# A three-stage kernel on one core: the last group's input combinations and the gate later, seven output pairs parked in HBM, two temporaries elsewhere

## The chip, the core and the metric

The kernel runs on one core of a Trainium2 chip. A core has TensorE (PE in the profile, with its weight loads as PEld), VectorE (DVE), ScalarE (ACT), GpSimd (POOL) and SyncE (SP, which here only issues DMAs). Each engine executes its own list of instructions in order and waits at semaphores for the others. The metric is the device time of one execution in microseconds (us). Three runs of the kernel before took 2025.17, 2027.48 and 2030.88 us, so the median is 2027.48 us.

## What is computed

Three layers follow each other on 2304 tokens of 512 values: a windowed attention, a rational two-layer network, and a mixture of 8 experts. The change lies in the third, of which the reference is:

```
logits = x @ w_gate                       # 2304 x 8
P = np.exp(logits - logits.max())
for _ in range(8):                        # the gate: rows and columns made even in turn
    P /= P.sum(1, keepdims=True) + 1e-09
    P /= P.sum(0, keepdims=True) + 1e-09
    P *= N / E
out = 0
for e in range(8):
    h = np.maximum(x @ w1[e], 0.0)        # 512 -> 1024
    ye = h @ w2[e]                        # 1024 -> 512
    out += P[:, e:e + 1] * ye
```

Every expert works on every token. P only scales the expert's output by rows, so the matrix products can begin before P is known; the scaled sum can't.

## The kernel before, in words

The tokens of the third layer form three groups G of 768. A visit v is one expert on one group; there are 24, experts outermost, the group order turning round at each expert (0 1 2, 2 1 0, ...). A visit has four steps m, each with a quarter of the hidden values, so there are 96 steps. Both matrix products use Strassen-like combinations: seven products take the place of eight. Each number is held as two 16-bit halves, so each product is three matmuls.

- **First layer** (`moe_l1`, matmuls at L925, banks `l1a` and `l1b`): step m has seven products at positions 0 to 6. One product is a unit u of the program: six matmuls of 384 columns. The units number 672, and 28 more follow for the second layer. ScalarE (L974, L981) and VectorE (L976, L979, L984) take results out of the two banks, VectorE and GpSimd combine them (L947), ScalarE rounds them to 16 bits (L991) and VectorE writes the rest (L992) to a tile `hs0` to `hs5`. A position that uses a bank again must wait until the result before it has been taken out.
- **Second layer** (`moe_l2`, matmuls at L1016 to L1018 of 256 columns, four banks `yps`): it begins 28 units later. After 28 products of three matmuls an output pair is complete (two blocks of 128 tokens). `y_evac` (L1036 to L1041) takes it out of the banks to one of two tiles, `yd0` and `yd1`, in turn. There are 72 pairs. The next pair needs the same four banks.
- **Output** (`y_out`): two ScalarE scalings by columns of P (L1050), then a store for expert 0 (L1053, SP's queue) or an adding DMA for the others (L1055, GpSimd's queue). Scaling needs the gate. Until the gate is done the pairs stand in a list, `pend`, and keep `yd0` and `yd1`.
- **Gate**: `x2_logits` (L766, L768 on TensorE) for each group, then `gate_exp`, eight times `gate_iter` (L787 to L796 on VectorE, with one column sum on TensorE, L180, read at L191), `gate_done` (L801).
- **Inputs**: the seven combinations of a group's x are made by `mix_sub` (L744) and `mix_put` (L222 and L225), written to HBM (`xd`, L754) and read from there (L911) as the steps need them. `x2f` held two combinations that later ones are made of.
- **Weights**: raw expert weights come in through two buffers (L838 and L844 to L846), are searched for their largest value (L850), combined (L874) and split into halves (L885, L888).

`at_u(u, f)` puts a piece of work at unit u of the program as written; a scheduler then orders each engine's list. All big tiles lie at fixed places (`homes`) in a few large rooms (`roomA`, `roomV`, `roomIG` in the profile), so two tiles at one place must wait for each other.

Of the kernel before, what the change touches and what calls it, by code (L numbers as in the profile page):

```python
# [10 lines left out]
F32 = mybir.dt.float32  # L11
F32R = mybir.dt.float32r
F16 = mybir.dt.float16
# [15 lines left out]
def kernel(  # L29
# [67 lines left out]
    homes(homes(homes(0, 7168, "w1s4", "V1", 2), 6144, "E03a", "V1", 2), 4096, "yd1", "V1", 2)  # L97
    homes(0, 10752, "hs0 hs1 hs2", "V2", 2)
    homes(0, 6144, "E47", "IG", 2)
    homes(7168, 3072, "mix4 mix5", "V0", 2)  # L100
    homes(0, 3072, "mix6 mix7", "V1", 2)
    rooms = {}
# [90 lines left out]
    def delayed(fn, k):  # L193
        return fn() if k == 0 else lambda: delayed(fn, k - 1)
# [539 lines left out]
            )  # L734

    def mix_src(G, c):
        if c in (CT1, CT2):
            return room("x2f", [P, 2, XQ], F32)[:, c == CT2, :]
        n, h = {CX00: (0, 0), CX10: (0, 1), CT4: (0, 1), CT3: (1, 0), CX11: (1, 1)}[c]
        return xhome(2 * G + n)[:, h * XQ:(h + 1) * XQ]  # L740
# [210 lines left out]
    def moe_unit(u):  # L951
        m, pos = divmod(u, 7)
        if pos == 1:
            m -= 1
        if not 0 <= m < NM:
            return
        if pos == 0:
            mac[m] = dict(
                A=bank("l1a"), E=room("E03" + "ab"[m % 2], [P, 4, TB], F32), D=room("E47", [P, 4, TB], F32),
            )  # L960
        d = mac[m]
        if pos == 3:
            d["Y"] = bank("l1b")
        ps = d["Y" if pos in (1, 3, 5) else "A"]
        if pos in (0, 3, 5):
            d[pos] = dict(ps=ps, used=0, guests=[])
        group = d[{0: 0, 2: 0, 4: 0, 6: 0, 3: 3, 5: 5, 1: 5}[pos]]
        moe_l1(m, pos, ps[:, 0:TB], group)
        if pos in (0, 5):
            fresh[:] = [group]  # L970
        ps = ps[:, 0:TB]
        E = d["E"]
        if pos in (0, 2, 4):
            nc.scalar.activation(E[:, (0, 2, 3)[pos // 2], :], ps, AF.Copy)  # L974
        elif pos == 3:
            nc.vector.tensor_tensor(out=E[:, 0, :], in0=ps, in1=E[:, 0, :], op=ALU.add)  # L976
            nc.scalar.activation(E[:, 0, :], E[:, 0, :], AF.Relu)
        elif pos == 5:
            nc.vector.tensor_tensor(out=E[:, 3, :], in0=ps, in1=E[:, 3, :], op=ALU.add)  # L979
        elif pos == 6:  # L980
            nc.scalar.activation(E[:, 1, :], ps, AF.Relu)  # L981
            combine(m, 6, 1, 0, ALU.subtract)
        else:
            nc.vector.tensor_tensor(out=E[:, 2, :], in0=ps, in1=E[:, 2, :], op=ALU.add)  # L984
            nc.scalar.activation(E[:, 2:4, :], E[:, 2:4, :], AF.Relu)  # L985
            combine(m, 4, 0, 2, ALU.add)
            combine(m, 5, 4, 1, ALU.subtract)
            combine(m, 7, 3, 5, ALU.subtract)
            h = d["h"] = room(f"hs{m % 6}", [P, 2, 7, TB], F16)
            for src, o in ((E[:, 1:4, :], slice(0, 3)), (d["D"], slice(3, 7))):  # L990
                behind["a"] = nc.scalar.activation(h[:, 0, o, :], src, AF.Copy).ins.name  # L991
                behind["v"] = nc.vector.tensor_tensor(out=h[:, 1, o, :], in0=src, in1=h[:, 0, o, :], op=ALU.subtract).ins.name  # L992
# [36 lines left out]
    def y_evac(v, p):  # L1029
        yd = room(f"yd{(3 * v + p) % 2}", [P, 2, DM], F32)  # L1030
        vv = room("yv", [P, EH], F32)
        p1, p6, _, _, _, _, p4 = (yb[b][:, h * EH:(h + 1) * EH] for b, h, _, _ in PRODS)
        p75, p23 = (yb[b].rearrange("p (n c) -> p n c", n=2) for b in (1, 2))
        q4 = yd.rearrange("p n (h c) -> p (n h) c", h=2)
        w, z, u, x = (q4[:, i, :] for i in range(4))
        nc.scalar.activation(u, p1, AF.Copy)  # L1036
        nc.vector.tensor_tensor(out=vv, in0=p6, in1=u, op=ALU.add)
        nc.vector.tensor_tensor(out=q4[:, 0:4:3, :], in0=p75, in1=vv.unsqueeze(1).to_broadcast([P, 2, EH]), op=ALU.add)
        nc.vector.tensor_tensor(out=z, in0=p75[:, 0, :], in1=x, op=ALU.add)  # L1039
        nc.vector.tensor_tensor(out=q4[:, 2:4, :], in0=p23, in1=q4[:, 2:4, :], op=ALU.add)  # L1040
        nc.vector.tensor_tensor(out=w, in0=p4, in1=w, op=ALU.add)  # L1041
        if gate_ready[0]:
            y_out(v, p, yd)
        else:
            pend.append((v, p, yd))

    def y_out(v, p, yd):
        e, G = GV[v]
# [5 lines left out]
        else:  # L1054
            later_u.append((unit_now[0] + 2, lambda: pin("p", nc.gpsimd.dma_start(out=dst, in_=yd, accum_op=ALU.add))))  # L1055

    def flush_pend():
        gate_ready[0] = True
        for a in pend:
            y_out(*a)  # L1060
        pend.clear()


    LAG = 3
    ATT = ((1, 0, 7), (2, 7, 23), (3, 40, 62))
# [67 lines left out]
    def at_u(u, fn, *a):  # L1133
        at(4 * NS1 + int(2 * u), fn, *a)
# [10 lines left out]
    def mix_at(G, when, s0, slot0):  # L1145
        for dt, c, slot in zip(s0, (CX00, CX10, CT1, CX11, CT2, CT3, CT4), (0, 1, 2, 3, 0, 1, 2)):
# [1 line left out]
                when(dt, mix_sub, G, c)  # L1148
            when(dt, mix_put, G, c, slot0 + slot)
            if c == CX11:  # L1150
                when(dt + (0.5 if G < 2 else 2), x2_logits, G)

    def at_step(t, fn, *a):
        at(int(4 * t) + 1, fn, *a)

    mix_at(0, at_step, (56, 57, 58, 59, 61, 62, 63), 0)
    mix_at(1, at_step, (69, 70, 71, 72, 74, 75, 76), 0)
    mix_at(2, at_u, (9, 12, 15.5, 19, 27.5, 30, 32.5), 4)
    for c in range(7):
        at_step(78 + c // 3, x_load, 0, c)  # L1160
    at_step(80.5, x_load, 1, CX00)

    at_u(23.5, gate_exp)
    for u in (26, 29, 32, 35, 38, 41, 44, 47):
        at_u(u, gate_iter)
    at_u(49, gate_done)
    at_u(49.5, flush_pend)

    use = []

# [174 lines left out]
```

## Time and profile before

| what | value |
|---|---|
| median of three runs | 2027.48 us |
| profiled execution, its own time | 2025.65 us |
| its span, first to last instruction | 2023.9 us |
| TensorE busy, share of the span | 1896.6 us, 94% |
| VectorE busy | 1625.1 us, 80% |
| ScalarE busy | 1235.8 us, 61% |
| GpSimd busy | 486.8 us, 24% |
| mean granted TensorE clock | 0.968 |
| first and last matmul of the first expert layer | 633.0 and 1986.2 us |

The third layer takes the span from 633 us to its end. A busy time says how long an engine had something to do; a matmul's record is longer than the distance to the next matmul, because they overlap, so TensorE's rate is read from counts and distances of starts, not from its busy share.

### The profile page before, as it was taken

What the parts mean: (1) busy time and instruction counts of PE and PEld (TensorE: products, weight loads), DVE (VectorE), ACT (ScalarE), POOL (GpSimd) and SP (SyncE); (2) the same over time, 40 slices, a digit from 0 to 9 for tenths busy, and PEclk for the clock granted to TensorE, in tenths of its full rate; (3) what the DMA queues carried; (4) which work ended last, traced back from release to release, by engine and by line L of the source; (5) the groups of instructions that cost most, each with busy time, mean ns of one, the idle gap of its engine ahead of it and who ended that gap; (6) DMA issues with size and microseconds to landing.
All of it is one profiled execution on the core that took longest, in us unless ns stands there. A gap on an engine that the chain in (4) does not pass through costs nothing. (4 is left out here: it accounts for less than half of the span.)

```text
span 2023.9 us, 36375 instructions
## 1 busy us (share of the span) xinstructions
PE 1896.6 (94%) x13914; PEld 1428.6 (71%) x13914; DVE 1625.1 (80%) x2784; ACT 1235.8 (61%) x2328; POOL 486.8 (24%) x490
## 2 busy tenths in 40 slices
PE   7688899998989789999999999999999999999997
PEld 6466667876766566777777777777777777777776
DVE  5898899899998878778877877878778787787754
ACT  5777777776776536565654655556566466565543
POOL 1232233222222003112411511421231241141111
PEclk7688999999999899999999999999999999999999
DMA  6642220124310333146346345435534634543323
GB/s 174 167 142 77 60 75 14 33 65 143 105 41 12 120 105 110 62 127 160 72 109 170 67 104 144 110 62 135 154 64 107 175 78 105 152 87 79 87 55 47
DMA packets 209791, 200.06 MB, mean 99 GB/s; under 512 B 78288, under 2 KB 160208, under 8 KB 209616
## 3 DMA queue, kind: packets, MB, share of 16 engines
q1 hardware_dynamic: 192480, 164.70, 26.9%
q0 software_dynamic: 17136, 33.03, 10.9%
q8 instruction: 109, 1.79, 0.4%
q14 instruction: 66, 0.54, 0.1%
HBM read 151.67 MB, written 46.01 MB: 98 GB/s over the span
## 5 line engine op out<-in xcount | busy, mean ns | idle before, releaser
L925 PEld LDWEIGHTS <-roomA 128*128 128x128 f16 x3276 | 321.9, 99 | 197.6 <-issue 32.2
L925 PE MATMUL l1a<-roomA 128*128 128x384 f16 x1872 | 358.8, 328 | 4.8 <-ACT roomV L974 3.7
L925 PE MATMUL l1b<-roomA 128*128 128x384 f16 x1404 | 277.3, 329 | 14.1 <-DVE roomA L976 6.7
L683 POOL TENSOR_TENSOR roomIG<-roomA,roomIG 128x384 fp32r<-128x384 f32 x96 | 112.2, 1169 | 289.2 <-ACT roomIG L682 214.8
L947 POOL TENSOR_TENSOR roomIG<-roomA 128x384 f32<-128x384 f32 x48 | 60.7, 1264 | 464.4 <-ACT roomA L981 314.1
L1016 PE MATMUL yps<-roomA,roomV 128*128 128x256 f16 x630 | 170.3, 274 | 2.0 <-DVE roomV L1039 1.3
L1016 PE MATMUL yps<-roomA 128*128 128x256 f16 x630 | 169.6, 273 | 2.5 <-DVE roomV L1040 1.5
L1017 PE MATMUL yps<-roomA,roomV 128*128 128x256 f16 x630 | 171.5, 274 | 0.0
L1017 PE MATMUL yps<-roomA 128*128 128x256 f16 x630 | 170.8, 273 | 0.0
L1018 PE MATMUL yps<-roomA,roomV 128*128 128x256 f16 x630 | 170.6, 274 | 0.0
L1018 PE MATMUL yps<-roomA 128*128 128x256 f16 x630 | 169.4, 273 | 1.0 <-DVE roomA L992 1.0
L645 PE MATMUL h1ps<-roomA 128*128 128x384 f16 x384 | 131.5, 343 | 15.4 <-DVE roomA L665 7.9
L698 PE MATMUL o1ps<-roomIG,roomV 128*128 128x384 f32 x384 | 137.1, 357 | 4.3 <-POOL roomIG L683 4.1
L874 POOL TENSOR_TENSOR roomA<-roomA 128x256 f32<-128x256 f32 x140 | 130.1, 948 | 37.3 <-DVE roomA L888 23.6
L646 PE MATMUL h1ps<-roomA 128*128 128x384 f16 x384 | 130.7, 340 | 0.0
L699 PE MATMUL o1ps<-roomIG,roomV 128*128 128x384 f32 x384 | 130.6, 340 | 0.0
L888 DVE SCALAR_TENSOR_TENSOR roomA<-roomA,sm 128x768 f16<-128x768 f32 (+1 forms) x92 | 113.7, 1249 | 21.1 <-ACT roomA L885 19.8
L647 PE MATMUL h1ps<-roomA 128*128 128x384 f16 x384 | 130.4, 339 | 0.0
L947 POOL TENSOR_TENSOR roomIG<-roomV 128x384 f32<-128x384 f32 x48 | 50.0, 1041 | 323.5 <-ACT roomV L981 304.7
L697 PE MATMUL o1ps<-roomIG,roomV 128*128 128x384 f32 x384 | 106.1, 377 | 15.9 <-ACT roomIG L682 14.2
L1016 PEld LDWEIGHTS <-roomA 128*128 128x128 f16 x1008 | 98.6, 98 | 30.6 <-DVE roomA L1040 3.7
L1017 PEld LDWEIGHTS <-roomV 128*128 128x128 f16 x1008 | 99.0, 98 | 25.0 <-issue 1.5
(221 smaller groups left out, 5081.6 us busy)
## 6 DMA issues: line engine op xcount, KB each, us to landing
roomA<-xd SPq DMA_DIRECT2D x119, 384.0 KB
roomA<-in_moe_w_dram SPq DMA_DIRECT2D x256, 128.0 KB
roomA<-in_moe_w_dram SPq DMA_DIRECT2D x128, 256.0 KB
out_dram<-roomV POOLq DMA_DIRECT2D x32, 512.0 KB, 6.0
out_dram<-roomA POOLq DMA_DIRECT2D x31, 512.0 KB, 6.1
roomV<-in_moe_w_in_dram SPq DMA_DIRECT2D x16, 512.0 KB
roomA<-in_moe_w_out_dram SPq DMA_DIRECT2D x16, 512.0 KB
xd<-roomA SPq DMA_DIRECT2D x14, 384.0 KB
```

The lines of the kernel that those rows point to most:

```text
L645: mm = nc.tensor.matmul(hp, whi, xb[:, 0, kk, :], start=kk == 0, stop=False)
L646: nc.tensor.matmul(hp, whi, xb[:, 1, kk, :], start=False, stop=False)
L647: nc.tensor.matmul(hp, wlo, xb[:, 0, kk, :], start=False, stop=kk == KD - 1)
L683: nc.gpsimd.tensor_tensor(out=gl, in0=g, in1=gh.bitcast(F32), op=ALU.subtract)
L698: nc.tensor.matmul(ob[dd], hi, d["gl"], start=False, stop=False)
L699: nc.tensor.matmul(ob[dd], lo, d["gh"], start=False, stop=last)
L874: pin("p" if pool else "v", eng.tensor_tensor(out=d[:, o, :], in0=a, in1=b, op=ALU.add if w == 0 and n == 0 else ALU.subtract))
L888: pin("v", nc.vector.scalar_tensor_tensor(out=l, in0=x, scalar=sc, in1=h, op0=ALU.mult, op1=ALU.subtract))
L925: mm = nc.tensor.matmul(ps, w[:, wx_, wh, kk * P:(kk + 1) * P], x[:, xh, kk, :], start=start and kk == 0 and wh == 0 and xh == 0, stop=sto ...
L1016: nc.tensor.matmul(o, hh[:, a - 1, c], w[:, m, 0, :], start=i == 0 and half == 0, stop=False)
L1017: nc.tensor.matmul(o, hh[:, a - 1, c], w[:, m, 1, :], start=False, stop=False)
L1018: nc.tensor.matmul(o, hl[:, a - 1, c], w[:, m, 0, :], start=False, stop=i == NP - 1 and (half == 1 or b == 3))
```

## The change

- `x2t1` and `x2t2` are new tiles for the two helper combinations of the last group, in place of `x2f`; one lies where `mix0` and `yd0` lie, the other where `yd1` lies.
- The units of the last group's seven combinations move a little (9 to 10, 12 to 13, 15.5 to 17, 19 to 21, 27.5 to 26, 32.5 to 34), and its logits from 2 to 5 units behind the fourth.
- The gate starts at unit 36 in place of 23.5, its eight turns stand at 41 to 89 in place of 26 to 47, and it is done at 94 in place of 49.
- Each output pair that is complete before the gate is stored unscaled to a tile `yh` in HBM at once. From unit 97 on, half a pair at a time, it is read back to one tile `yr`, scaled by ScalarE and stored to the output. There are seven such pairs and so fourteen turns, two in seven units.
- The tiles `hs4` and `hs5` change their order of use.

```diff
+    homes(0, 3072, "x2t1")
+    homes(13312, 3072, "x2t2", "V1", 2)
+    homes(14336, 2048, "yr", "V0", 2)
...
+        if c in (CT1, CT2) and G == 2:
+            return room("x2t2" if c == CT2 else "x2t1", [P, XQ], F32)
...
-            h = d["h"] = room(f"hs{m % 6}", [P, 2, 7, TB], F16)
+            h = d["h"] = room(f"hs{(0, 1, 2, 3, 5, 4)[m % 6]}", [P, 2, 7, TB], F16)
...
-            pend.append((v, p, yd))
+            i = len(pend)
+            nc.sync.dma_start(out=yh[:, 2 * DM * i:2 * DM * (i + 1)], in_=yd.rearrange("p n c -> p (n c)"))
+            pend.append((v, p, i))
...
-    def flush_pend():
+    yh = hbm.tile([P, 8 * 2 * DM], F32, tag="yh", name="yh")
+
+    def flush_one(k):
+        v, p, i = pend[len(pend) - 1 - k // 2]
+        n = k % 2
+        e, G = GV[v]
+        assert e == 0
+        yr = room("yr", [P, DM], F32)
+        pin("a", nc.sync.dma_start(out=yr, in_=yh[:, DM * (2 * i + n):DM * (2 * i + n + 1)]))
+
+        def done():
+            pin("a", nc.scalar.activation(yr, yr, AF.Copy, scale=gate_col(e, 2 * TPB * G + TPB * n + p)))
+            nc.sync.dma_start(out=bass.AP(out.tensor, (2 * TPB * G + TPB * n + p) * P * DM, [[DM, P], [1, DM]]), in_=yr)
+
+        return delayed(done, 5)
+
+    def flush_pend(u):
         gate_ready[0] = True
-        for a in pend:
-            y_out(*a)
-        pend.clear()
+        for k in range(2 * len(pend)):
+            at_u(u + 2 + 7 * (k // 2) + 3 * (k % 2), flush_one, k)
...
-                when(dt + (0.5 if G < 2 else 2), x2_logits, G)
+                when(dt + (0.5 if G < 2 else 5), x2_logits, G)
...
-    at_u(23.5, gate_exp)
-    for u in (26, 29, 32, 35, 38, 41, 44, 47):
+    at_u(36, gate_exp)
+    for u in (41, 47, 53, 65, 71, 77, 83, 89):
         at_u(u, gate_iter)
-    at_u(49, gate_done)
-    at_u(49.5, flush_pend)
+    at_u(94, gate_done)
+    at_u(95, flush_pend, 95)
```

In the changed kernel the line numbers of the pieces below are 3 higher up to the gate's column sum (L191 becomes L194), and 5 higher from the logits to the second layer (L766 becomes L771, L1016 becomes L1021). L1051 is the store to `yh`, L1072 the load of `yr`, L1076 the store to the output.

TensorE's list at the last group's logits before, from the last logit matmuls of 16 columns on:

```order
L766 LDWEIGHTS roomV_6434
L766 MATMUL lgps<-wg,roomV_6434 128x16
L768 LDWEIGHTS roomV_6434
L768 MATMUL lgps<-wg,roomV_6434 128x8
L768 LDWEIGHTS roomV_6434
```

and the same place now (`yps` are the banks of the second layer):

```order
L771 LDWEIGHTS roomV_6435
L771 MATMUL lgps<-wg,roomV_6435 128x16
L1022 LDWEIGHTS roomV_6694
L1022 MATMUL yps<-roomA,roomV_6694 128x256
L773 LDWEIGHTS roomV_6435
L773 MATMUL lgps<-wg,roomV_6435 128x8
```

Matmuls of the second layer now stand between the logits; before, the first of them stood behind the gate's first column sum. From the logits to position 3 of step 4 there are 42 of them now and none before.

VectorE's list at the gate's first turns before (`gs` and `gt` are the gate's tiles):

```order
L888 SCALAR_TENSOR_TENSOR roomA<-roomA,sm 128x4x256
L191 TENSOR_SCALAR gs<-smps 128x8
L992 TENSOR_TENSOR roomA<-roomIG,roomA 128x1536
L794 RECIPROCAL gs<-gs 128x8
L795 TENSOR_SCALAR gs<-gs 128x8
L796 TENSOR_TENSOR gt<-gt,gs 128x144
L787 TENSOR_REDUCE gs<-gt 128x18
L788 TENSOR_SCALAR gs<-gs 128x18
L789 RECIPROCAL gs<-gs 128x18
L790 TENSOR_TENSOR gt<-gt,gs 128x144
L792 TENSOR_REDUCE gs<-gt 128x8
```

and in the first turn now (L1042 to L1046 take out the first output pair):

```order
L795 TENSOR_TENSOR gt<-gt,gs 128x144
L1042 TENSOR_TENSOR roomA<-yps,roomA 128x256
L797 TENSOR_REDUCE gs<-gt 128x8
L1043 TENSOR_TENSOR roomA<-yps,roomA 128x2x256
L981 TENSOR_TENSOR roomV_6584<-l1b,roomV_6584 128x384
L1044 TENSOR_TENSOR roomA<-yps,roomA 128x256
L1046 TENSOR_TENSOR roomA<-yps,roomA 128x256
L997 TENSOR_TENSOR roomA<-roomIG,roomA 128x1536
L984 TENSOR_TENSOR roomA<-l1b,roomA 128x384
L1045 TENSOR_TENSOR roomA<-yps,roomA 128x512
L855 TENSOR_REDUCE sm<-roomA 128x1 x2
L194 TENSOR_SCALAR gs<-l1b 128x8
```

The gate's turn now stands spread among the work of the expert layers.

SyncE's list where the first output was stored before:

```order
L911 DMA roomA<-xd 128x1536
L1053 DMA out_dram<-roomA 128x2x512
L1053 DMA out_dram<-roomV_6583 128x2x512
L844 DMA roomA<-in_moe_w_dram 128x256
L845 DMA roomA<-in_moe_w_dram 128x256
L846 DMA roomA<-in_moe_w_dram 128x512
```

and one of the fourteen turns now (`yh` is the parked pair, `roomV_6435` the tile `yr`):

```order
L849 DMA roomA<-in_moe_w_dram 128x256
L850 DMA roomA<-in_moe_w_dram 128x256
L851 DMA roomA<-in_moe_w_dram 128x512
L1072 DMA roomV_6435<-yh 128x512
L916 DMA roomA<-xd 128x1536 x2
L1076 DMA out_dram<-roomV_6435 128x512
```

The load of `yr`, and behind ScalarE's scaling the store from it, stand in one list with the loads of weights (L849 to L851) and inputs (L916).

## Rows read from the trace of the kernel before

**Rows 1.** The page's busy times and clock: share of the span, instructions.
```profile
PE 1896.6 (94%) x13914; PEld 1428.6 (71%) x13914; DVE 1625.1 (80%) x2784; ACT 1235.8 (61%) x2328; POOL 486.8 (24%) x490
```
**Rows 2.** Stretches: length; busy us (count) of PE, PEld, DVE, ACT, POOL; clock, DMA, GB/s.
```profile
660.00:700.00 40.00, 29.59 (x206) 18.32 (x205) 38.74 (x67) 25.33 (x34) 4.29 (x3) 0.79 0.44 152
740.00:770.00 30.00, 22.40 (x114) 12.53 (x114) 24.07 (x44) 15.77 (x24) 2.00 (x2) 0.77 0.60 192
660.00:830.00 170.00, 149.47 (x1088) 105.51 (x1087) 137.41 (x252) 86.98 (x124) 32.12 (x31) 0.91 0.33 109
```
**Rows 3.** The same for line L925, first layer: busy PE, PEld; clock, DMA, GB/s.
```profile
660.00:700.00 40.00, 22.98 (x118) 12.01 (x116) 0.79 0.44 152
740.00:770.00 30.00, 20.01 (x91) 10.26 (x90) 0.77 0.60 192
660.00:830.00 170.00, 86.76 (x448) 45.82 (x446) 0.91 0.33 109
1000.00:1985.00 985.00, 549.71 (x2979) 291.19 (x2977) 1.00 0.45 106
```
**Rows 4.** The same for tile yps, second layer: busy PE, DVE, ACT; clock, DMA, GB/s.
```profile
660.00:700.00 40.00, 4.56 (x24) 0.00 (x0) 0.00 (x0) 0.79 0.44 152
740.00:770.00 30.00, 2.05 (x19) 1.10 (x2) 0.37 (x1) 0.77 0.60 192
660.00:830.00 170.00, 68.32 (x558) 15.12 (x30) 2.25 (x6) 0.91 0.33 109
1000.00:1985.00 985.00, 554.27 (x4483) 137.39 (x270) 20.18 (x54) 1.00 0.45 106
```
**Rows 5.** TensorE's timeline: start, duration, line, tiles, count, idle before and its releaser.
```profile
655.38 2.11 PE L925 MATMUL l1a<-roomA 128*128 128x384 f16 x12
...
670.58 0.22 PE L768 MATMUL lgps<-wg,roomV 128*128 128x8 f16 x2 [0.54 <-DVE roomV L225]
...
693.28 2.08 PE L925 MATMUL l1b<-roomA 128*128 128x384 f16 x6 [6.67 <-DVE roomA L976]
...
734.11 0.27 PE L1018 MATMUL yps<-roomV,roomA 128*128 128x256 f16 x1
...
735.09 0.27 PE L1018 MATMUL yps<-roomV,roomA 128*128 128x256 f16 x1
...
754.84 2.08 PE L925 MATMUL l1b<-roomA 128*128 128x384 f16 x6 [3.33 <-DVE gs L191]
```
**Rows 6.** The same for the gate's tile gs: busy PE, PEld, DVE, ACT; clock, DMA, GB/s.
```profile
660.00:700.00 40.00, 0.82 (x4) 1.01 (x4) 4.47 (x17) 0.41 (x1) 0.79 0.44 152
685.00:760.00 75.00, 2.54 (x16) 2.87 (x16) 19.20 (x73) 0.41 (x1) 0.89 0.27 84
```
**Rows 7.** ScalarE's timeline at the third output pair, and at a store's landing.
```profile
672.09 0.94 ACT L222 ACTIVATE roomV<-roomA,sm 128x768 f16<-128x768 f32 x1 [0.64 <-DMA xd<-roomV]
...
764.10 0.37 ACT L1036 ACTIVATE roomA<-yps 128x256 f32<-128x256 f32 x1
...
771.39 0.72 ACT L1050 ACTIVATE roomA<-roomA,pwt 128x512 f32<-128x512 f32 x1
```
**Rows 8.** VectorE's and GpSimd's timelines at weight preparation and the gate's end.
```profile
689.21 1.75 DVE L888 SCALAR_TENSOR_TENSOR roomA<-roomA,sm 128x768 f16<-128x768 f32 x1
776.89 1.01 DVE L888 SCALAR_TENSOR_TENSOR roomV<-roomA,sm,roomV 128x768 f16<-128x768 f32 x1
688.50 1.65 POOL L947 TENSOR_TENSOR roomIG<-roomA 128x384 f32<-128x384 f32 x1 [10.53 <-DVE roomV L992]
753.49 1.22 DVE L850 TENSOR_REDUCE sm<-roomA 128x1 f32<-128x1024 f32 x1 [2.91 <-DMA roomA<-in_moe_w_dram]
758.41 0.23 DVE L1025 TENSOR_SCALAR pwt<-pe__7482,sm 128x18 f32<-128x18 f32 x1
```
**Rows 9.** SyncE's timeline: issues of stores of inputs and loads of weights.
```profile
667.75 4.05 SPq L754 DMA_DIRECT2D xd<-roomV  x4
...
750.69 0.43 SPq L846 DMA_DIRECT2D roomA<-in_moe_w_dram  x1
```

More of the change, by code (lines that the diff above doesn't have):

```diff
@@ L1157 @@
     mix_at(1, at_step, (69, 70, 71, 72, 74, 75, 76), 0)
-    mix_at(2, at_u, (9, 12, 15.5, 19, 27.5, 30, 32.5), 4)
+    mix_at(2, at_u, (10, 13, 17, 21, 26, 30, 34), 4)
     for c in range(7):
```

## The prediction, as it was put down before the changed kernel had run

> **What bounds the kernel now.** I read the page's busy times first. TensorE is at 94% of the span, VectorE at 80% [rows 1]; so the question is where TensorE loses time, and the view by stretches answers it. TensorE's rate is counted, not taken from its busy share. Twelve first-layer matmuls in a row take 2.11 us with the last one's 0.33, so one follows another after 0.162 us; nine distances between second-layer matmuls, from 734.11 to 735.09, give 0.109 us [rows 5]. In the long middle part, 1000 to 1985 us, 2979 × 0.162 + 4483 × 0.109 = 971 us, with 20 small side matmuls some 973 of 985: only 1.2% is lost there [rows 3, 4]. That part can't get faster without less work, and the change takes no matmul away.
>
> The stretch 660 to 830 us, where the expert layer starts, is another matter. 448 × 0.162 + 558 × 0.109 = 133.4 us [rows 3, 4], and with the 60 logit matmuls (some 3 us) and the side matmuls (2 us) 138.6 of 170 us: 31 us are lost. At the middle part's 1.2% it would lose 2, so about 29 us is the most that can be won. Nearly all lies at two places. From 660 to 700: 118 × 0.162 + 24 × 0.109 + 4 = 25.7 of 40 us, 14.3 lost. From 740 to 770: 91 × 0.162 + 19 × 0.109 + 0.4 = 17.2 of 30 us, 12.8 lost. These are also two stretches with a low granted clock, 0.79 and 0.77 [rows 2], where the middle part has 1.00 [rows 3]: after a wait of 6.67 us six first-layer matmuls took 2.08 us, and after one of 3.33 us again 2.08 us [rows 5], twice the distance of the 12 above, so TensorE ran at 1.2 in place of 2.4 GHz. A wait is paid here a second time.
>
> **Why it waits at the first place.** VectorE is busy 38.74 of 40 us there [rows 2], with mixing, weights, hidden values and gate in one list; the gate's part is 4.47 us [rows 6]. TensorE has first-layer work only, and each product needs its bank taken out by that full VectorE.
>
> **Why at the second.** The third output pair's matmuls end at 735.20, behind the row at 735.09 [rows 5], but its evacuation begins at 764.10 [rows 7], 29 us later: `yd0` and `yd1` still hold the first two pairs, the gate's column is only there at 758.41 [rows 8], and scaling and storing come after it. So the second layer stands (19 matmuls in 30 us [rows 4]), the first layer runs alone, at half of TensorE's work for one unit of VectorE's, and VectorE's queue with the gate's turns in it sets the pace. The 3.33 us wait is one for a gate instruction.
>
> **The change, part by part.** All sums go against the profiled execution's own 2025.65 us (span 2023.9 and 1.75 around it); the median of the runs is 1.83 above it.
>
> Logits and the first place. By their order, the mixing instructions hardly move, so "later" costs and gives next to nothing by itself. What moves is that 42 second-layer matmuls, 4.6 us, now stand between the logits and position 3 of step 4, where TensorE only waited. VectorE has no less to do at this place but for part of the gate's 4.47 us. So I don't let all 14.3 us go. I leave 0.5 us for the last wait among the logits (0.54 [rows 5]), 1.7 for a bank that ScalarE takes out behind a long rounding, and 3.4 for the first pair's evacuation, whose five VectorE instructions now stand between hidden-value work. I checked the last by adding up: from the end of L976 in step 4 on, VectorE's list to the last evacuation of the first pair sums to 21 us of instructions, TensorE's list to the first matmul that needs it to 23 us. VectorE is ahead by some 2 us, and must not be late by more. Left: 5.6 us; won: 8.7.
>
> Parking the pairs. A pair leaves `yd` when its store to HBM has landed. The nearest row: input combinations stored from 667.75 on gave their tile back at 672.09 [rows 9, 7], so 4 us or less for 384 KB, and as an estimate 5 us for 512 KB. A tile is needed again after two pairs, 2 × 28/3 units; a unit takes 985 / (2979/6) = 1.98 us [rows 3], so 37 us. The store is hidden with 32 us to spare, and the second layer never stands. The gate's turns, 19.2 us of VectorE between 685 and 760 [rows 6], spread over units 36 to 94, 115 us. I leave 3 of the 12.8 us: won 9.8.
>
> What becomes late next: VectorE. The stretch holds 137.4 us of its work [rows 2]; if the stretch shrinks from 170 to some 153 us, that is 90% in place of 81%. The gate's later turns move to where pairs and weights are worked on. I charge 1 us. Summing both lists up to the gate's end, VectorE stays 1 to 10 us ahead of TensorE at nearly every bank, never behind; but at 90% each wait of its own for ScalarE or a DMA (2.91 us at 753.49 [rows 8]) shows.
>
> The fourteen turns. ScalarE's scalings are as many as before (14 of them, 0.72 us in the row [rows 7]), SP gets 7 stores, 14 loads and 7 more output stores, at 0.4 us each 11 us over 190 us of a queue that mostly waits. `yr` is one tile, so each turn is a chain: load, scaling, store, landing, next load. On ScalarE the scaling stands in the middle of the list; if the load is late, bank evacuations behind it wait, and TensorE for them. On SP, weight and input loads stand behind the stores. No row shows such a turn. From below: no cost, since the load is issued 2.5 units, 5 us, ahead. From above: the weights' last load, issued 750.69 and done by 753.49 [rows 9, 8], took 2.4 us behind its 0.43; if ScalarE stood for all of that at each turn, 14 × 2.4 = 33.6 us. I take 0.1 us a turn, 1.5 us in all, nearest to the lower end, since in the middle part such loads land under cover.
>
> The new places of `x2t1`, `x2t2` and the exchange of `hs4` and `hs5` take away waits on one place; the walk above has none left at either, and I put nothing for it. The added 7.3 MB over some 190 us are 38 GB/s, beside the 93 to 192 that these stretches move [rows 2]: nothing.
>
> Sum: 8.7 + 9.8 − 1 − 1.5 = 16 us. 2025.65 − 16 = 2009.65, and with the 1.83 to the median **2011 us**.
>
> **A rule weighed.** A VectorE instruction of 768 columns took 1.75 us where GpSimd was at work (688.50 for 1.65 us), another of the same shape 1.01 us where it was not [rows 8]. The Trainium skill's page "GPSIMD Engine Reference", section "1. Specifications", says that GpSimd shares its SBUF interfaces with VectorE and is in contention with instructions that have two SBUF inputs. This pair of rows agrees. By that rule a fuller VectorE meets GpSimd's 32.12 us [rows 2] more often: 9 points more of it, at 0.74 us for 1.65, would be 1.3 us of VectorE's time and as much less won, 2012 us.
>
> **The rivals.**
>
> *VectorE holds the pace.* For it: at the first place VectorE is at 97% and TensorE starves. Against it: the two lists' sums. If VectorE can't be driven beyond 81 to 86% when its work hangs on two other engines, 137.4 us need 160 to 170 us, and 0 to 10 us are won; with the 2.5 charged, 2020 to 2030, middle 2025.
>
> *The parked pairs hold ScalarE.* This is the case on the other side. A turn by rows: 0.33 issue, 2.4 landing, 0.72 scaling, 0.38 issue, up to 4 for the store, 7.8 us; fourteen take 110 us, and the turns are laid into 53 units, 105 us. So the chain may run late by itself, and late loads stop ScalarE in its list. At 2.4 us a turn, 2011 − 1.5 + 33.6 = 2043 us. It decides from (18.5 − 1) / 14 = 1.25 us a turn on: there nothing is left of the gain. Against it: ScalarE is busy 61% [rows 1], so part of a stop is made up before TensorE feels it.
>
> By the Trainium skill's "DMA: Bandwidth & Descriptors", section "Anatomy of one DMA — SWDGE (gpsimd) path", a DMA costs about 2.0 us and its bytes at 436 GB/s. An estimate from it is 2.6 us for each 256 KB here and 6.6 us for a turn; the chain would then have 12 us to spare and this rival would fall. No run here shows it yet.
>
> *More is won.* If the clock stays at full speed all through and the three waits I left at the first place don't come, 24 to 27 us go: 2000 to 2003.
>
> *It does not do what it says* is excluded for the parking, which the lists show; for the later combinations it holds, as said.
>
> **How the numbers follow.** Forecast 60%, own range 2003 to 2018; more won 10%; VectorE holds the pace 20%; the turns hold ScalarE 10%. A measurement of this kernel tells about 0.3%, 6 us, from no change: faster is below 2021.4, slower above 2033.6. Faster: 0.59 + 0.10 + 0.06 from VectorE's better half = 0.75. Same: 0.01 + 0.13 + 0.02 = 0.16. Slower: 0.01 + 0.08 = 0.09. For 8 in 10 the range goes from 2001, inside the case of more won, to 2026, which takes in most of VectorE's.
>
> **What would show it.** Right: from 660 to some 815 us the same 448 and 558 matmuls; clock 1.00 or near it in each 20 us from 680 on; no stretch of 20 us without second-layer matmuls after 700; VectorE near 90%. Wrong: a wait of TensorE above 3 us and a low clock anywhere up to 830 (first place not healed); ScalarE waiting at L1075 for a DMA, above all more than 1 us a time, between 830 and 950; SP's weight loads late behind L1072 or L1076, seen as waits at L850 or L885 (L855 and L890 in the changed kernel) for a DMA; or L1016's matmuls waiting for evacuations, which would mean that VectorE is behind after all.

## The result, and the profile after

The changed kernel took 2010.9 us (median of 4 runs, 2005.36 to 2012.21) where the kernel before took 2027.51 beside it (4 runs, 2025.17 to 2030.88): 0.9912 of its time, 95% interval 0.9888 to 0.9935. The forecast was 2011. The profiled execution is the run of 2012.21 us, span 2010.4; line numbers are 3 to 7 higher than before.

The page's busy times, as in [rows 1]: the instructions are the same in number on TensorE and VectorE, and VectorE is busy 3.7 us less.

```profile
PE 1897.6 (94%) x13914; PEld 1430.5 (71%) x13914; DVE 1621.4 (81%) x2784; ACT 1234.9 (61%) x2328; POOL 484.4 (24%) x490
```

The stretches of [rows 2]: length, busy us (count) of PE, PEld, DVE, ACT, POOL; clock, DMA share, GB/s.

```profile
660.00:700.00 40.00, 37.44 (x293) 24.13 (x292) 37.64 (x59) 28.92 (x41) 4.73 (x4) 1.00 0.45 152
740.00:770.00 30.00, 30.00 (x235) 22.77 (x233) 28.08 (x62) 15.01 (x21) 6.78 (x8) 1.00 0.43 132
660.00:830.00 170.00, 165.49 (x1272) 120.62 (x1271) 151.68 (x279) 95.02 (x134) 32.31 (x34) 0.99 0.35 115
```

The same for the first layer, now L930, as in [rows 3] (busy PE; clock, DMA, GB/s):

```profile
660.00:700.00 40.00, 29.75 (x175) 1.00 0.45 152
740.00:770.00 30.00, 17.02 (x89) 1.00 0.43 132
660.00:830.00 170.00, 99.79 (x547) 0.99 0.35 115
```

and for the second layer's tile, as in [rows 4] (busy PE, DVE, ACT; clock, DMA, GB/s):

```profile
660.00:700.00 40.00, 7.29 (x54) 0.00 (x0) 0.00 (x0) 1.00 0.45 152
740.00:770.00 30.00, 17.70 (x138) 3.65 (x7) 0.36 (x1) 1.00 0.43 132
660.00:830.00 170.00, 81.58 (x641) 17.75 (x35) 2.63 (x7) 0.99 0.35 115
```

In 170 us there are 547 and 641 matmuls in place of 448 and 558. By the prediction's count the first place now loses 40 − (175 × 0.162 + 54 × 0.109 + 3.4) = 2.4 us in place of 14.3, the second 30 − (89 × 0.162 + 138 × 0.109 + 0.3) = 0.2 in place of 12.8. VectorE is busy 94% at both and TensorE is fed; the clock, 0.79 and 0.77 before, is 1.00.

The changed execution starts its expert layer 4.6 us later, so the stretches don't hold quite the same work. At the same distance from the start the first place of before is 655.4 to 695.4 us (L925, busy PE; clock, DMA, GB/s):

```profile
655.40:695.40 40.00, 27.52 (x145) 0.84 0.44 152
```

With no second-layer matmul there it lost 40 − (145 × 0.162 + 4) = 12.5 us. So some 10 us were won at this place: 54 second-layer matmuls, 5.9 us, and 30 more of the first layer, 4.9 us.

What VectorE was relieved of shows in the gate's tile, as in [rows 6]:

```profile
660.00:700.00 40.00, 0.38 (x2) 0.35 (x2) 0.56 (x2) 0.00 (x0) 1.00 0.45 152
685.00:760.00 75.00, 1.53 (x10) 1.66 (x10) 10.03 (x37) 0.41 (x1) 1.00 0.46 150
```

TensorE's timeline has the waits that are left, beside [rows 5]: two of 1 and 2 us early, and two late that weren't there before.

```profile
694.23 1.14 PE L930 MATMUL l1a<-roomA 128*128 128x384 f16 x6 [1.05 <-ACT roomV L979]
...
784.65 1.68 PE L930 MATMUL l1a<-roomA 128*128 128x384 f16 x6 [1.95 <-ACT roomV L979]
...
931.65 1.14 PE L930 MATMUL l1a<-roomA 128*128 128x384 f16 x6 [1.75 <-ACT roomA L979]
...
938.65 2.08 PE L930 MATMUL l1a<-roomA 128*128 128x384 f16 x6 [2.49 <-ACT roomA L979]
```

The late two hang on the turns. ScalarE's timeline just there: it stands at the scaling L1075 until the load of `yr` has landed, and the evacuation L979, for which TensorE waits, stands behind it in the list. For the second wait two of ScalarE's other instructions, L990 and L996, stand between.

```profile
923.70 0.72 ACT L1075 ACTIVATE roomV<-roomV,pwt 128x512 f32<-128x512 f32 x1 [3.92 <-DMA roomV<-yh]
...
930.12 0.72 ACT L1075 ACTIVATE roomV<-roomV,pwt 128x512 f32<-128x512 f32 x1 [4.22 <-DMA roomV<-yh]
930.75 0.47 ACT L986 ACTIVATE roomV<-l1a 128x384 f32<-128x384 f32 x1
931.12 0.48 ACT L979 ACTIVATE roomA<-l1a 128x384 f32<-128x384 f32 x1
...
935.58 0.72 ACT L1075 ACTIVATE roomV<-roomV,pwt 128x512 f32<-128x512 f32 x1 [2.35 <-DMA roomV<-yh]
...
938.13 0.47 ACT L979 ACTIVATE roomA<-l1a 128x384 f32<-128x384 f32 x1
```

SyncE's list shows the first turn's load and the last turns: load, 4 to 5 us to the store, 2 to 2.5 us to the next load.

```profile
828.41 0.33 SPq L1072 DMA_DIRECT2D roomV<-yh  x1
...
919.85 0.34 SPq L1072 DMA_DIRECT2D roomV<-yh  x1
924.45 0.36 SPq L1076 DMA_DIRECT2D out_dram<-roomV  x1
...
926.95 0.41 SPq L1072 DMA_DIRECT2D roomV<-yh  x1
930.87 0.36 SPq L1076 DMA_DIRECT2D out_dram<-roomV  x1
...
932.91 0.32 SPq L1072 DMA_DIRECT2D roomV<-yh  x1
```

ScalarE's waits at L1075, from 800 to 965 us (us in total, times, longest):

```profile
ACT roomV L1075 <- DMA roomV<-yh: 21.2, 9, 4.2
```

VectorE stands for a turn, too. The third expert's column of P (L1030) takes the place of the first expert's, `pwt`, which the last turn's scaling still reads:

```profile
DVE pwt L1030 <- ACT roomV L1075: 5.8, 1, 5.8
```

This wait ends at 936.33 us. VectorE's next instruction waits for ScalarE until 937.06 us in any case, so no part of the loss can be put down to it alone.

To place gains and losses by progress, I cut each profiled execution at two matmuls that stand in every trace. *Start* is when the expert layer's first matmul (L925, L930) starts. *Front* is from there to the start of the 751st second-layer matmul; both places lie in it, and in the changed kernel three of the fourteen turns. *Rest* is from there to the start of TensorE's last matmul; the other eleven turns lie in it.

```
kernel                        start   front    rest    median of the runs
before                        633.1   238.4  1142.3    2027.5
after                         637.7   212.9  1149.8    2010.9
gate early, parked            635.7   232.2  1142.5    2024.3
only gate and parking         638.8   210.9  1152.5    2008.8
no turns                      634.5   211.0  1143.7    2000.5
turns 5 units apart           634.6   211.0  1148.5    2008.2
  the same, scaled later      638.0   210.9  1152.1    2010.1
  and gate late but packed    633.3   222.9  1142.1    2012.1
gate from 30, not parked      633.0   227.6  1143.3    2019.7
turns issued by ScalarE       633.8   211.0  1149.9    2007.6
turns at light times          637.6   210.9  1145.0    2005.4
small turns                   634.0   210.9  1146.0    2005.7
after, once more              631.3   211.2  1151.9    2007.8
five pairs                    634.9   215.1  1144.0    2005.6
```

("The same, scaled later" is the kernel with turns 5 units apart; "and gate late" is built on it.) From before to after: start +4.6, front −25.5, rest +7.5, together −13.4; the spans differ by 13.5.

### The profile page after: what moved, and what is told of

It reads as the page before. It is cut to its first block, busy times and chain, and to the rows that moved or that the text cites. A ratio compares the mean times of both kernels' runs of the same rounds, so it can differ in the third digit from the quotient of the medians.

```text
span 2010.4 us, 36420 instructions
## 1 busy us (share of the span) xinstructions
PE 1897.6 (94%) x13914; PEld 1430.5 (71%) x13914; DVE 1621.4 (81%) x2784; ACT 1234.9 (61%) x2328; POOL 484.4 (24%) x490
## 5 line engine op out<-in xcount | busy, mean ns | idle before, releaser
L930 PEld LDWEIGHTS <-roomA 128*128 128x128 f16 x3276 | 320.1, 98 | 184.7 <-issue 18.2
L930 PE MATMUL l1a<-roomA 128*128 128x384 f16 x1872 | 358.9, 327 | 9.0 <-ACT roomA L979 4.5
L930 PE MATMUL l1b<-roomA 128*128 128x384 f16 x1404 | 273.5, 326 | 2.1 <-DVE roomV L981 1.2
L1021 PE MATMUL yps<-roomA 128*128 128x256 f16 x630 | 170.4, 274 | 2.5 <-DVE roomV L1045 1.5
L1021 PE MATMUL yps<-roomA,roomV 128*128 128x256 f16 x630 | 168.8, 273 | 0.1
L701 PE MATMUL o1ps<-roomIG,roomV 128*128 128x384 f32 x384 | 139.2, 363 | 4.8 <-POOL roomIG L686 4.7
L702 PE MATMUL o1ps<-roomIG,roomV 128*128 128x384 f32 x384 | 132.6, 345 | 0.0
L893 DVE SCALAR_TENSOR_TENSOR roomA<-roomA,sm 128x768 f16<-128x768 f32 (+1 forms) x92 | 112.9, 1240 | 19.4 <-ACT roomA L890 18.2
L700 PE MATMUL o1ps<-roomIG,roomV 128*128 128x384 f32 x384 | 106.8, 379 | 15.4 <-ACT roomIG L685 13.7
L1021 PEld LDWEIGHTS <-roomA 128*128 128x128 f16 x1008 | 98.9, 98 | 30.6 <-DVE roomA L1045 3.4
L1021 PEld LDWEIGHTS <-roomV 128*128 128x128 f16 x1008 | 98.8, 98 | 24.2 <-DVE roomA L1044 0.5
```

What stands on the lines that cost most here:

```text
L701: nc.tensor.matmul(ob[dd], hi, d["gl"], start=False, stop=False)
L702: nc.tensor.matmul(ob[dd], lo, d["gh"], start=False, stop=last)
L893: pin("v", nc.vector.scalar_tensor_tensor(out=l, in0=x, scalar=sc, in1=h, op0=ALU.mult, op1=ALU.subtract))
L930: mm = nc.tensor.matmul(ps, w[:, wx_, wh, kk * P:(kk + 1) * P], x[:, xh, kk, :], start=start and kk == 0 and wh == 0 and xh == 0, stop=sto ...
L1021: nc.tensor.matmul(o, hh[:, a - 1, c], w[:, m, 0, :], start=i == 0 and half == 0, stop=False)
```

## The experiments

**What mends the front: gate early, but parked.** In the changed kernel the gate, logits and mixing go back to the units of before:

```diff
-    at_u(36, gate_exp)
-    for u in (41, 47, 53, 65, 71, 77, 83, 89):
+    at_u(23.5, gate_exp)
+    for u in (26, 29, 32, 35, 38, 41, 44, 47):
...
-    at_u(95, flush_pend, 95)
+    at_u(49.5, flush_pend, 49)
```

> The changed kernel with the gate, the logits and the mixing back at the units of before (gate from 23.5 to 49, pairs scaled from unit 51 on); parking, the two temporaries and the exchange of hs stay. Only two pairs are parked then. Theory (parking mends the second place, spreading the gate mends the first): the first place from 660 to 700 us loses some 14 us as before, the second nothing; 2025 to 2027 less 10 to 12, so 2015 to 2018 us. Rival (parking alone gives all of it): 2009 to 2012 us. Rival (VectorE with the gate's turns packed into 685 to 760 still sets the pace there): 2022 us or more.

Measured: 2024.31 us, ratio 0.998 (0.9971 to 0.9989). The third account is the nearest: parking alone wins 6.2 us of the front, and the second place isn't mended, since by the count some 8 us are lost from 740 to 780 us. That VectorE with the packed gate sets the pace there is not shown: TensorE's longest waits there are for ScalarE, 1.7 and 1.3 us, and ScalarE itself stands 4.5 us for loads of the four turns that now fall near this place. At the first nothing is changed; the wait of 6.67 us of [rows 5] is there again:

```profile
695.83 2.08 PE L930 MATMUL l1b<-roomA 128*128 128x384 f16 x6 [6.67 <-DVE roomA L981]
```

**Only gate and parking.** The mixing times, the logits' distance, the two temporaries and the exchange of `hs` go back:

```diff
...
-                when(dt + (0.5 if G < 2 else 5), x2_logits, G)
+                when(dt + (0.5 if G < 2 else 2), x2_logits, G)
...
-    mix_at(2, at_u, (10, 13, 17, 21, 26, 30, 34), 4)
+    mix_at(2, at_u, (9, 12, 15.5, 19, 27.5, 30, 32.5), 4)
```

> The changed kernel with the last group's mixing times, the logits' distance, the two temporaries and the exchange of hs back as before; only the later gate and the parking are left of the change. Theory of the prediction (places give nothing, but the 42 second-layer matmuls, 4.6 us, that the later logits bring between give something at the first place): 2013 to 2016 us. Rival (gate and parking are all that counts): 2010 to 2012 us. Rival (the waits on the one place of the temporaries are what held the first place): 2019 us or more.

Measured: 2008.75 us, ratio 0.991 (0.9893 to 0.9928), front 210.9. The rival that gate and parking are all that counts is the nearest, and the time lies below even its range: those parts give nothing that can be measured. My price for the logits' distance was wrong too; the second layer starts 33.2 us behind the first without it, as in the changed kernel (33.3; before 62.3).

**Gate from 30, nothing parked.** The kernel before, with one edit:

```diff
-    at_u(23.5, gate_exp)
-    for u in (26, 29, 32, 35, 38, 41, 44, 47):
+    at_u(29.5, gate_exp)
+    for u in (33, 35, 37, 39, 41, 43, 45, 47):
```

> The kernel before (no parking, nothing else changed), with the gate's exponential at unit 29.5 and its turns at units 33 to 47 in place of 23.5 and 26 to 47; its end stays at 49. In the list the second layer's first matmul then stands ahead of the gate's maximum and first column sum. Theory (this place in TensorE's list is what costs at the first place): the second layer starts some 33 us behind the first, not 62, the first place loses 3 to 6 us in place of 14, while the second pair of the second place still waits for the gate: 2017 to 2022 us. Rival (the first place is VectorE's fullness with the gate's turns, which are denser here): 2026 us or more. Rival (what is won at the first place is lost at the second, since the pairs must wait for the gate's end all the same): 2026 to 2029 us, with more than 20 us lost from 740 to 790 us.

Measured: 2019.72 us, ratio 0.9959 (0.9943 to 0.9974). The theory holds: the second layer starts 33.2 us behind the first, the front is 10.8 us shorter, and the first place keeps clock 1.00 though VectorE is fuller than in the changed kernel:

```profile
660.00:700.00 40.00, 36.19 (x293) 23.91 (x291) 38.88 (x64) 26.49 (x37) 4.63 (x4) 1.00 0.46 152
```

VectorE's work for the gate hardly fell there, 4.06 us on the tile `gs` in place of 4.47 [rows 6], and its evacuation L976 started at 692.83 us, where it had been 692.69; but TensorE waited 0.18 us for it in place of 6.67, since it had other matmuls to do. So at the first place it was the position of the gate's maximum and first column sum in TensorE's list, ahead of all second-layer work, which gave TensorE nothing to do while VectorE was full. What remains is the second place: from 740 to 760 us there are 21 second-layer matmuls, and TensorE stands, by the row, for the store of a pair:

```profile
752.54 1.44 PE L925 MATMUL l1a<-roomA 128*128 128x384 f16 x6 [3.62 <-DMA out_dram<-roomA]
```

**No turns.**

```diff
+            dst = bass.AP(out.tensor, (2 * TPB * G + p) * P * DM, [[DM, P], [TPB * P * DM, 2], [1, DM]])
-            nc.sync.dma_start(out=yh[:, 2 * DM * i:2 * DM * (i + 1)], in_=...)
+            nc.sync.dma_start(out=dst, in_=yd)
...
-            at_u(u + 2 + 7 * (k // 2) + 3 * (k % 2), flush_one, k)
```

> The changed kernel without the turns: the seven parked pairs are stored unscaled straight into the output and never loaded, scaled or stored again (their scaling by the gate is left out). Theory (the turns cost the 7 us lost from 910 to 960): 2003 to 2006 us, no loss there. The prediction's own price of the turns, 1.5 us: 2009 to 2010 us. Rival (that loss is not the turns'): 2011 us with the waits still there.

Measured: 2000.51 us, ratio 0.9869 (0.9851 to 0.9887), rest 1143.7; the time is below even the theory's range. Against this one profiled execution the turns cost the changed kernel 6.1 and 8.2 us of the rest in its two profiled executions, and 7 to 10 us by the medians, not the 1.5 of the prediction.

**Turns 5 units apart**, then **scaled later** as well:

```diff
-            at_u(u + 2 + 7 * (k // 2) + 3 * (k % 2), flush_one, k)
+            at_u(u + 2 + 5 * k, flush_one, k)
...
-        return delayed(done, 5)
+        return delayed(done, 7)      # in the second of the two only
```

> The changed kernel with the fourteen turns every 5 units (10 us) over units 97 to 162, in place of 3 and 4 units apart over 97 to 142. Theory (the 7 us that TensorE loses from 910 to 960 us come from turns of about 6 us that are laid 6 and 8 us apart, so that the load comes late and ScalarE stands at L1075): ScalarE's waits there fall from 21 us to under 5, 2004 to 2007 us. Rival (the loss is the mere work of the turns or another wait in that stretch): 2010 to 2012 us.

> The changed kernel with the fourteen turns 5 units apart (as in the run with wide turns, 2008.2 us, where ScalarE still waited 16.7 us in 9 waits at L1075) and the scaling laid 3.5 units behind its load in place of 2.5. Theory (what is left of the turns' price, 7.7 us against the run without turns, is ScalarE standing at L1075 for late loads): these waits go under 5 us and the time falls to 2001 to 2004 us. Rival (the price is SP's list: the load waits there for the store before it, and weight loads stand behind both): 2007 to 2010 us, with SP's waits at L1072 and L1076 unchanged.

Measured: 2008.2 us, ratio 0.9901 (0.9887 to 0.9915), and 2010.12 us, ratio 0.9912 (0.9895 to 0.9928). Both miss the theory: ScalarE's waits stay at 16.7 and 15.1 us. The load isn't issued when its unit comes; in the second kernel, from 830 to 1000 us, SyncE holds it until the store before it has landed (us in total, times, longest), and all that is behind it in SyncE's list too:

```profile
SPq L1072 <- DMA out_dram<-roomV: 19.6, 8, 5.0
```

**Turns issued by ScalarE.** As the last, with `nc.scalar.dma_start` for load and store of `yr`:

> The run with wide turns and scalings 3.5 units behind, and the turns' loads and stores issued by ScalarE in place of SP. Theory (SP's list is what is left of the price: weight loads stand behind loads and stores of the turns that wait): 1 to 3 us faster than that run, and no wait of weights for a DMA between 850 and 960 us. Rival (it is ScalarE's own waits): no faster, since ScalarE now also waits before each load for the store's landing; the same or 1 to 5 us slower.

Measured: 2007.59 us, ratio 0.9897 (0.9879 to 0.9915), 2.5 us less than issued by SyncE, rest 2.2 us less. It fits the theory, but the intervals overlap and the rest of one kernel scatters by as much; and ScalarE now stands for the stores instead:

```profile
893.94 0.49 ACT L986 ACTIVATE roomV<-l1a 128x384 f32<-128x384 f32 x1 [4.71 <-DMA out_dram<-roomV]
```

**Gate late, but packed**, on the kernel with turns scaled later; three pairs are parked:

```diff
-    for u in (41, 47, 53, 65, 71, 77, 83, 89):
+    for u in (40.5, 42.5, 44.5, 46.5, 48.5, 50.5, 52.5, 54.5):
...
-    at_u(95, flush_pend, 95)
+    at_u(57.5, flush_pend, 57)
```

> The run above, and the gate's eight turns packed: from unit 36 to 57 in place of 36 to 94, so that only three pairs are parked and six turns run. Theory (VectorE has no room for the gate's 19 us in 21 units, 42 us, at 80% other work): 8 to 11 us are lost between 700 and 770 us, six turns in place of fourteen give some 3 to 4 back; 2009 to 2013 us. Rival (only the gate's start behind the second layer's first matmul matters, spreading does nothing): 2000 to 2004 us.

Measured: 2012.13 us, ratio 0.9918 (0.9902 to 0.9934). The time is as the theory says: the front is 12.0 us longer, TensorE waits for a gate instruction, and the rest, with no turn in it, is 1142.1.

```profile
740.53 0.59 PE L183 MATMUL l1a<-gs,sm 128*128 128x8 f32 x2 [1.82 <-DVE gs L797]
```

But its reason, that VectorE has no room, doesn't show. In the 20 us where TensorE loses most, VectorE (the third busy time) works 15.3 us, and in the 20 before them 15.8:

```profile
740.00:760.00 20.00, 18.47 (x101) 11.19 (x101) 15.32 (x44) 7.44 (x13) 1.00 (x1) 0.83 0.41 116
```

From 700 to 780 us it waits 3.8 us for TensorE's column sums, so the two engines wait for each other in the gate's turns; how the 12.0 us divide was not traced.

**Turns at light times.** The turns move to units where the run without turns leaves room in the DMA engines. At the place that they leave, that run's two stretches from 900 us on (last two columns: DMA share, GB/s) are

```profile
900.00:910.00 10.00, 10.00 (x77) 7.33 (x76) 7.26 (x11) 5.36 (x9) 1.20 (x2) 1.00 0.68 222
910.00:920.00 10.00, 9.91 (x80) 7.62 (x79) 7.47 (x15) 5.05 (x7) 1.00 (x1) 1.00 0.62 148
```

and in the changed kernel, with turns there, they are full:

```profile
900.00:910.00 10.00, 9.99 (x77) 7.28 (x76) 6.75 (x12) 5.15 (x9) 0.00 (x0) 1.00 0.99 324
910.00:920.00 10.00, 9.81 (x78) 7.40 (x77) 8.72 (x11) 7.46 (x11) 2.20 (x2) 1.00 1.03 301
```

```diff
-        for k in range(2 * len(pend)):
-            at_u(u + 2 + 7 * (k // 2) + 3 * (k % 2), flush_one, k)
+        for k, t in enumerate((97, 101, 105, 109, 119, 123.5, 153, 157.5, 162, 166.5, 177, 181, 186, 190)):
+            at_u(t, flush_one, k)
...
-        v, p, i = pend[len(pend) - 1 - k // 2]
+        v, p, i = pend[(6, 3, 4, 5, 0, 1, 2)[k // 2]]
```

> The changed kernel with the fourteen turns laid to units where the run without turns shows the DMA engines little busy: ten at 97 to 109, 119, 123.5, 153 to 166.5 and four at 177 to 190, none between 124 and 152, where weights and inputs of the second expert are loaded (there the DMA share is 0.62 to 0.89 without turns, and 0.99 and 1.03 with them). The pairs are taken in the order in which the second expert adds to them. Theory (the turns' price of some 8 us is the DMA engines' saturation from 880 to 930 us: loads and stores of a turn land late there, and weights and inputs too): 2001 to 2004 us, no wait at L1075 over 3 us. Rival (each turn costs by its chain through SP and ScalarE wherever it stands): 2007 to 2011 us.

Measured: 2005.36 us, ratio 0.9871 (0.9851 to 0.9891), 1.4 us over the theory's range; its profiled execution started late (637.6). By front and rest the fourteen turns cost 1.2 us together. ScalarE still waits at L1075, once for more than the 3 us that the theory allowed, but TensorE doesn't feel it:

```profile
ACT roomV L1075 <- DMA roomV<-yh: 10.3, 6, 3.3
```

**Small turns**, at the places of the changed kernel:

```diff
-        pin("a", nc.sync.dma_start(out=yr, in_=yh[:, ...]))
+        pin("a", nc.sync.dma_start(out=yr[:, 0:16], in_=yh[:, ...]))
...
-            nc.sync.dma_start(out=bass.AP(..., [[DM, P], [1, DM]]), in_=yr)
+            nc.sync.dma_start(out=bass.AP(..., [[DM, P], [1, 16]]), in_=yr[:, 0:16])
...
+        nc.gpsimd.memset(room("yr", [P, DM], F32), 0.0)
```

> The changed kernel, turns at their places, with loads and stores of 16 columns in place of 512 (most of the seven pairs' output is left out); SP's instructions, the chain of waits and ScalarE's scalings of 512 columns stay. Theory (the price is the traffic at a saturated place): 2000 to 2004 us, ScalarE's waits at L1075 under 8 us in all in place of 21. Rival (the price is the number of instructions and waits in SP's and ScalarE's lists): 2007 to 2011 us.

Measured: 2005.68 us, ratio 0.9883 (0.9865 to 0.9902), between the two; rest 1146.0, 2.3 us over that without turns. ScalarE's waits fell only from 21.2 to 16.0 us, against the theory:

```profile
ACT roomV L1075 <- DMA roomV<-yh: 16.0, 9, 4.7
```

So by the rest some 2 us of the price are the chain of instructions and waits, and 4 to 6 come only with the turns' traffic at that place. This split isn't firm: by the medians it is 5 and 2 to 5 us, and the rest of one kernel scatters by 2.1 us. Full DMA engines alone didn't cost TensorE anything: with turns at light times the share is 1.00 from 900 to 910 us as well, and TensorE starts 77 matmuls there, as without turns. Nor are ScalarE's waits alone a measure: 16.0 us of them went with 2.3 us of the rest, 21.2 us with 6.1.

In the changed kernel's two profiles most of what TensorE waits from 830 to 1010 us is for ScalarE's L979, 4.4 and 5.8 us, and no wait is for a load of weights, so nothing there shows weights that land late. VectorE's wait at L1030, 5.8 and 7.5 us in the two, is gone with small turns and with turns 5 units apart; as the rest is hardly shorter in the latter (1148.5, and 1152.1 scaled later), it is not the main part of the price, but its share was not separated.

**After, once more, and five pairs.** The first is unaltered; the second is the kernel with turns at light times, ten in place of fourteen, and

```diff
-    at_u(36, gate_exp)
-    for u in (41, 47, 53, 65, 71, 77, 83, 89):
+    at_u(30, gate_exp)
+    for u in (34, 39.5, 45, 50.5, 55.5, 65, 70, 75):
...
-    at_u(94, gate_done)
+    at_u(79, gate_done)
```

> The changed kernel once more, unaltered, beside the next one on the same chip, since the profiled executions of all kernels so far differ by up to 5.8 us (633.0 to 638.8) in when the first product of the expert layer starts, where their lists are alike. If this is only scatter, its median is 2008 to 2012 us, and in the profile the time from the 750th second-layer matmul to TensorE's end stays near 1150 us, whatever the start. If the variation belongs to single kernels, this profile's start lies within 0.5 us of the first one's 637.7.

> The kernel with the turns at light times (2005.4 us), and the gate from unit 30 to 79 in place of 36 to 94, its turns about 5.5 units apart: five pairs are parked, ten turns run, eight of them at units 82 to 119 and two at 153 and 157.5. Theory (turns at light times are nearly free, and VectorE has room for the gate at this distance): the same within 3 us, 2002 to 2007 us. Rival (VectorE has no room at 5.5 units a turn, as it had none at 2): a loss of 3 to 8 us between 700 and 790 us, 2008 us or more.

Measured: 2007.8 us, ratio 0.9891 (0.9876 to 0.9905), and 2005.56 us, ratio 0.9881 (0.9864 to 0.9897). The one kernel started at 637.7 and at 631.3, while front and rest agree within 2.1 us: the start is scatter. The second is as fast as the kernel with seven pairs at light times: its front, in which six of the ten turns lie, is 4.2 us longer, part of it a wait for the gate, its rest 1.0 shorter.

```profile
758.69 2.08 PE L930 MATMUL l1a<-roomA 128*128 128x384 f16 x6 [1.94 <-DVE gs L194]
```

The two best, 2005.4 and 2005.6, lie below both medians of the changed kernel, but their intervals overlap that of its second run; what is clear of the scatter is the rest, 1145.0 and 1144.0 against 1149.8 and 1151.9.

## Why the prediction was right, point by point

The time was right to less than 1 us (the sum gives 2011.5), which is luck in part: two terms were mis-sized in opposite directions, and scatter of the start is larger than that. Measured again, the same kernel was 23.0 us faster than the one before beside it (2007.8 and 2030.8), not 16.6.

- *The bound.* Right. All that was won lies in the front, where TensorE was starved, and the waits and the low clocks at both places went together. One low stretch is left in the front, a mean of 0.91 from 780 to 800 us, behind the wait of 1.95 us.
- *First place, 8.7 us.* The sign was right, the size too small: 11.9 by the same count, some 10 at the same distance from the start, since 2.4 and not 5.6 us stay. Of the three waits left there on paper, the logits' is there (0.57 us at 673.79) and ScalarE's (1.05 at 694.23); the first pair's evacuation, 3.4, never came late: VectorE's small lead of 2 us in the lists was enough. What won it is in the larger part what the lists showed, second-layer matmuls where TensorE only waited; why 30 more of the first layer fit in as well was not traced. It isn't the later logits that bring them there, as the prediction's wording suggests: the gate's shift does it, even in the kernel before (10.8 us of the front).
- *Second place, 9.8 us.* 12.6 by the same count. Parking gives little by itself (6.2), and gate and parking belong together: parked pairs let the gate be late and spread. Packed into 21 units, the late gate lost 12.0 us.
- *VectorE, −1 us.* The two places and this term made 17.5 us; front measured 25.5 and 27.2. So 8 to 10 us too little. Its share of 660 to 830 us, 89%, is as forecast. The rival that VectorE holds the pace falls: at 94% it fed TensorE at both places. The packed kernel isn't this rival either, since VectorE was busy under 80% from 720 to 760 us there.
- *The turns, −1.5 us.* The step that was too low: the eleven in the rest cost 6.1 to 8.2 us there, so 0.55 to 0.75 us each in place of 0.1. It failed at two sentences: that the added traffic is nothing, taken from a mean of 38 GB/s, where from 880 to 920 us, without any turn, loads of weights and inputs already take 0.62 to 0.76 of the engines; and that a load issued 2.5 units ahead lands under cover, where SyncE holds it for the store before. The turns' place was read wrong, too: the loads are laid at units 97 to 142, so 45 units or 89 us from first to last, not 53 units and 105 us; measured are 104.5 us, from 828.41 to 932.91, so the chain ran some 15 us late. The rival named this mechanism with its place, and its point of decision, 1.25 us a turn, was not reached.
- *The later combinations, the temporaries, the exchange of `hs`: 0.* Right, by the kernel without them.
- *The rule on GpSimd and VectorE.* The Trainium skill's page "GPSIMD Engine Reference", section "1. Specifications", has GpSimd in contention with VectorE instructions of two SBUF inputs. From a pair of rows I had weighed 1.3 us that a fuller VectorE would lose by it. The busy total went from 1625.1 [rows 1] to 1621.4 us for the same 2784 instructions, and from 660 to 830 us the mean instruction took 0.545 us before and 0.544 after, so no such loss shows.
- *The rule on DMA time.* From the fixed cost and the bandwidth of one transfer in the Trainium skill's page "DMA: Bandwidth & Descriptors", section "Anatomy of one DMA — SWDGE (gpsimd) path", I had estimated 6.6 us a turn and 12 us to spare. The last two distances from load to load are 7.1 and 6.0 us, near the estimate, though the turns go through SyncE; but all thirteen lie between 5.6 and 11.7 us, 8.0 in the mean. In the 89 us that the units give, the estimate left 3 us to spare, not 12, and the conclusion that the rival falls didn't follow.

Sum in the profiled executions: 17.5 − 1.5 = 16 was forecast; 25.5 − 7.5 − 4.6 of the start = 13.4 came, and 27.2 − 9.6 + 1.8 = 19.4 in the second one, whose start was early.

## What to carry to other kernels

A wait far down the list can be made by what stands at its head: look for work that the waiting engine could do meanwhile, and move the serial side job behind it. Space that lets a result be late is worth more than its own wait, because it lets the job that it waited for be spread; and a transfer put off must be priced against the DMA share of the very stretch where it lands, not a mean, and with the waits of all that stands behind it in each engine's list. Where two executions of one kernel differ by as much as the effect, cut the trace at fixed instructions and compare the pieces.

## What the hardware showed that was not expected

The start of the expert layer varied from 631.3 to 638.8 us in 14 profiled executions, 6.4 us of it between two of one kernel; the stretches at a granted clock of 0.50 (1.2 GHz) ahead of it differ, in all 13.7 to 23.9 us from 300 to 640 us, but not in step with the start (17.1 us of them for 633.1 and for 638.8), so its cause stays open. And transfers of a 32nd of the size left 16.0 of 21.2 us of ScalarE's waits, so most of these hang on the chain of issue and landing and not on the bytes.
